# Half slots of a routed expert layer: second product with the tokens as rows, one step later, and both token loads moved among the full slots

## The chip, the cores and the metric

The kernel runs on one core of a Trainium2 chip. The metric is the device time of one execution in microseconds (us). The engines are TensorE (PE, its weight loads PEld), VectorE (DVE), ScalarE (ACT), GpSimd (POOL) and SyncE (SP), which issues nearly all DMAs here. Each engine works through its own queue in the order of the program.

## The reference

Three layers follow one another over 2304 tokens of width 512:

```
attn = softmax(scale*q k^T + bias, causal) v                    # 4 x 8 heads, 576 positions, 64 wide
e    = argmax(x w_gate + modality_bias);  p = softmax(...)[e]   # x: the heads side by side
h    = relu(x[mask] w1[e]);  moe[mask] = p * (h w2[e])          # 8 experts, 512 -> 1024 -> 512
out  = (sigmoid(moe wg) * (moe wv)) wo                          # 512 -> 1536 -> 512
```

With the reference's inputs (seed 0) the router sends 1191 rows to one expert, 1097 to a second, 16 to a third and none to the others.

## The kernel before, in words

**Slots.** After the attention, each expert's rows are cut into full slots of 256 rows; a rest of at most 128 rows becomes a half slot. There are nine full slots (MAIN, the last is slot 8) and two half slots (MAINH, numbered 32 and 33) in the straight path; here that makes five and four full slots and two half slots with 16 and 73 rows, so 2215 rows lie in full slots. More slots than that are done in `extras` (L1070) behind a branch on the register `more`, which the router computes (L822 to L826). `more` is also set when fewer rows than a threshold lie in full slots (L824).

**A full slot** has eight steps (`Moe.step`, L1154), one for each 128 columns of the hidden layer. A step is a first product of 12 matmuls (`mm1`, L989), a Relu on ACT (L993) with the low part `hL` on DVE (L994), and the second product of the step before (`mm2`, L1009). Values are kept as a high and a low part, so that each product is three matmuls. After each step `aheads` splits the weights for three steps ahead (`split_piece`, L922 and L925): two casts on ACT, one subtraction on DVE, one on POOL. Steps are counted from the end of the full slots: step 0 is the first step of the half slots, step -1 the last of slot 8, and each of the negative steps takes about 2.85 us.

**A half slot** has four steps k (`half`, L1111) in plain float32, where the program's one matmul is two passes in the records. A step transposes the hidden part of the step before (`half_t`: PE L1093, copy to `hT` on DVE L1095), makes the first product (`phh`, L1116: eight passes of 256 columns), a Relu on ACT (L1118), and then the second product of the step before (`half_mm2`, L1104: sixteen passes of 128 columns, with the weights `raw` standing in the array and the tokens streaming). The result has the 512 features on the partitions, as the store wants it. After k = 3, `store` (L1015) copies it to `yt` on ACT (L1021) and issues two DMAs on SP: the result to the DRAM tensor `x2` (L1023) and the row numbers to `ids2` (L1031). `half_x` (L1080) transposes the tokens of the next half slot (`htr`), one step of k = 2 of the first or step -2.

**Weights of the half slots.** `load_raw` (L897) loads part a (w1, L902) and part b (w2, L904) of quarter k into the tile pair `raw[k]`. In `Moe.run` (L1190), after half step i, part b of step i - 1 and part a of step i are loaded for the second half slot; a load waits until the product that reads the old contents is done.

**Around the steps.** `main` puts tasks of the third layer (`Moe2`) at steps by `put(step, tasks)`, and `step(u)` runs them after step u. `load_x(t)` (L1258) loads 768 columns of `x2` in four DMAs: t = 0 into tiles `xs`, t = 1 into `xt`. `x_tasks` (L1269, `sums` at L1272) are 18 tasks on such a load: seven casts on ACT (L1277), seven subtractions for low parts (L1278) and four sums (L1279) on DVE. Before, t = 0 is loaded at step -7 and its tasks run three a step at steps -4 to 1; t = 1 is loaded at step 0, and its tasks, with the split of the third layer's first weights (`w_tasks`, L1302 to L1324), run at steps 2 to 8. `preload` (L1242) brings the table for Sigmoid onto ACT, at step 8. Behind step 8 stands the branch over `extras` (L1072), and then `Moe2.run`, which loads t = 2 and starts the third layer's matmuls (L1342).

Of the kernel before, what the change touches and what calls it, by code (L numbers as in the profile page):

```python
# [8 lines left out]
F32 = mybir.dt.float32  # L9
# [6 lines left out]
ALU = mybir.AluOpType  # L16
# [10 lines left out]
BP, BT, WARM = 3, 3, 16  # L27
# [27 lines left out]
class Attention:  # L55
    def __init__(self, tc, ctx, ps, q, k, v, s, ident, new_x, on_batch, tick):
        self.tc, self.nc = tc, tc.nc
        self.q, self.k, self.v, self.s = q, k, v, s
        self.ident = ident
        self.new_x, self.tick = new_x, tick  # L60
        self.on_batch = on_batch
        self.B, self.H, self.S, self.D = q.shape
        self.N = self.B * self.H
        P = lambda n, b, **kw: ctx.enter_context(tc.tile_pool(name=n, bufs=b, **kw))
        self.cp = P("a_const", 1)
        self.wgx = self.cp.tile([128, 4, 144], F32, name="wgx")
        self.wk = P("a_work", 2)
        self.ps = ps
        self.sb = ps.tile([128, 1024], F32, name="sb")
        self.side, self.beside, self.reads = [], None, {}  # L70
        self.in_ctx = ExitStack()
        self.inp = self.in_ctx.enter_context(tc.tile_pool(name="a_in", bufs=2, side="right"))
        self.dr = P("a_dram", 1, space=DRAM)
        self.raw, self.kv, self.hd, self.bias_t, self.oT, self.sums = {}, {}, {}, {}, {}, {}
        self.x, self.pr, self.nr, self.cumB, self.qtt = {}, {}, {}, {}, {}
        self.setup()
# [400 lines left out]
    def run(self, late):  # L477

        pairs = self.N // 2
        last = pairs + max(e[2] for e in PERIOD) - 1  # L480

        def issue(nm, p, par):
            self.emit(nm, p, par)
            if nm[0] in "TALNR" or nm in ("evql", "qksl"):
                self.tick()

        for op in START:
            nm, n = op.split("@")
            issue(nm, int(n) // 2, int(n) % 2)
        for w in range(3, last + 1):  # L490
            for nm, par, sh in PERIOD:
                if 0 <= w - sh < pairs:
                    if (last - w, nm, par) in late:
                        late[last - w, nm, par]()
                    issue(nm, w - sh, par)
# [6 lines left out]
MAINH, HALVES, HROW, NROW = 2, 8, 32, 40  # L502


class Router:
# [240 lines left out]
    def slots(self):  # L746
# [5 lines left out]
        nc, T, q = self.nc, self.T, self.q  # L752
        V = nc.vector
# [4 lines left out]
        cmp, X = (self.fill[:, a : a + 9 * k].rearrange("p (a b) -> p a b", b=9) for a, k in ((0, 8), (72, 4)))  # L758
        A, B, C, nt, inc, E, Z = t9("sA"), t9("sB"), t9("sC"), t9("nt"), t9("inc"), t9("sE"), t9("sZ")
        n1 = lambda nm, dt=F32: T([128, 1], nm, dt)  # L760
        es, ep, s0, el, ch, g1, ex, z, base, void = (n1(nm) for nm in ("es", "ep", "s0", "el", "ch", "g1", "sx", "sz", "base", "void"))
# [3 lines left out]
        op = lambda f, *a, **kw: q.append(lambda: f(*a, **kw))  # L765
# [55 lines left out]
        op(V.tensor_copy, tt, inc[:64, 8:9])  # L821
        op(V.tensor_reduce, s0[0:1], W[0:1, 1], axis=AX.X, op=ALU.add)  # L822
        op(V.tensor_scalar, s0[0:1], s0[0:1], float(MAINH), None, ALU.is_gt)
        op(V.tensor_scalar, void[0:1], X[0:1, 3, 0:1], 4.0 * Moe2.G, None, ALU.is_lt)  # L824
        op(V.tensor_tensor, s0[0:1], s0[0:1], void[0:1], ALU.max)
        op(V.scalar_tensor_tensor, out=more, in0=inc[0:1, 8:9], scalar=float(MAIN), in1=s0[0:1], op0=ALU.is_gt, op1=ALU.max)  # L826
        q.append(lambda: self.indices("idx", self.tid, NROW, self.B * self.S - 1))
# [54 lines left out]
class Moe:  # L882
    def __init__(self, tc, raw, ps, acc, router, w1, w2, x, x2, ids2, ident):
        self.tc, self.nc = tc, tc.nc
        self.acc, self.x2, self.ids2 = acc, x2, ids2
        self.raw, self.ps, self.r, self.w1, self.w2, self.x, self.ident = raw, ps, router, w1, w2, x, ident
        self.xg, self.xT, self.y, self.piece, self.regs = {}, {}, {}, {}, {}
        self.prev, self.hprev, self.pend, self.ready = None, None, [], False
        self.wbufs = 24

    def open(self, ctx, early):
# [163 lines left out]
    def simple_half(self, s):  # L1055
        self.gather(s)
        self.gate(s)
        self.half_x(s)
        for k in range(4):
            self.load_slot(s, k)  # L1060
            self.half(s, k)
        self.half_end()
# [35 lines left out]
    def half_mm2(self, s, k, t):  # L1098
        nc = self.nc
        if k == 0:  # L1100
            self.y[s] = [self.ps.tile([128, 512], F32, tag="tr", name="yh", bufs=BT)]
        for dc in range(4):
            for j in range(2):
                nc.tensor.matmul(  # L1104
                    self.y[s][0][:, 128 * dc : 128 * dc + 128], self.raw[k][1][:, j, 128 * dc : 128 * dc + 128],
                    t[:, 128 * j : 128 * j + 128], start=k + j + dc == 0, stop=k == 3 and j == 1 and dc == 3, skip_group_check=True,
                )
        if k == 3:
            self.store(s)

    def half(self, s, k):  # L1111
        nc = self.nc
        ready = self.half_t(*self.hprev) if self.hprev else None
        ph = self.ps.tile([128, 512], F32, tag="pt", name="phh", bufs=BP)[:, :256]
        for dc in range(4):
            nc.tensor.matmul(ph, self.xT[s][:, dc], self.raw[k][0][:, dc], start=dc == 0, stop=dc == 3)  # L1116
        h = self.wk.tile([128, 256], F32R, tag="hH", name="hh", bufs=4).bitcast(F32)
        nc.scalar.activation(h, ph, AF.Relu)  # L1118
        if ready:
            self.half_mm2(*ready)  # L1120
        self.hprev = (s, k, h)

    def half_end(self):
        self.half_mm2(*self.half_t(*self.hprev))
        self.hprev = None

    LE, LA = 2, 3

# [61 lines left out]
    def run(self, step):  # L1190
        for u in range(8 * EARLY, 8 * MAIN):
            self.next()
            step(u)
            self.aheads(self.LA)
        for i in range(4 * MAINH):
            s, k = HROW + i // 4, i % 4
            self.half(s, k)
            if i == 0:
                self.finish()
                for h in range(1, MAINH):  # L1200
                    self.gate(HROW + h)
            elif k == 2 and s + 1 < HROW + MAINH:
                self.half_x(s + 1)
            for part, j in (("b", i - 1), ("a", i)):
                if 0 <= j < 4 * (MAINH - 1):
                    self.load_slot(HROW + j // 4 + 1, j % 4, part)
            step(8 * MAIN + i)
        ready = self.half_t(*self.hprev)
        self.hprev = None
        self.half_mm2(*ready)  # L1210
        step(8 * MAIN + 4 * MAINH)


# [510 lines left out]
def kernel(ctx, tc, q, k, v, s, modality_id, moe_w_gate, modality_bias, w1, w2, wg, wv, wo, out):  # L1724
    nc = tc.nc
    B, H, S, D = q.shape
    pool = lambda c, n, b=1, **kw: c.enter_context(tc.tile_pool(name=n, bufs=b, **kw))
    cp = pool(ctx, "const")
    dr = pool(ctx, "dram", space=DRAM)
    x = dr.tile([B * S, RW], F32, name="x")  # L1730
# [4 lines left out]
    with tc.manual_schedule():  # L1735
        ident = cp.tile([128, 128], F32, name="ident")
        make_identity(nc, ident)
        ps_ctx, at_ctx, mo_ctx, ea_ctx, mw_ctx, ex_ctx, xs_ctx, wo_ctx, x1_ctx = (ExitStack() for _ in range(9))
# [42 lines left out]
        phase, more, keep = [0], [], []  # L1781
# [19 lines left out]
        glu = Moe2(tc, moe, x2, ids2, wg, wv, wo, out, hd, keep[0], rp, wo32)  # L1801
        todo, last, xs, raws, x1, raws1 = {}, 8 * MAIN, [], [], [], []

        def put(at, tasks):
            todo.setdefault(at, []).extend(tasks)
# [13 lines left out]
        put(-6, [lambda: moe.gate(HROW)])  # L1819
        put(-2, [lambda: moe.half_x(HROW)])  # L1820
        put(0, [mw_ctx.close])
        put(-7, [lambda: glu.load_x(0, raws), lambda: glu.room_x(0, keep[0])])

        def open_second():
            glu.second = pool(ctx, "second", reuse_waits="tile")
            glu.room_x(1, glu.second)
            x1.append(pool(x1_ctx, "x_second", side="right", reuse_waits="tile"))
            raws1.extend(x1[0].tile([128, 2, glu.G], F32, name=f"xt{i}") for i in range(4))
            glu.load_x(1, raws1)

        put(0, [open_second])

        def first_tokens():
            x = glu.x_tasks(0, raws)
            for k in range(6):
                put(k - 4, x[3 * k : 3 * k + 3])

        def later():
            x, cuts = glu.x_tasks(1, raws1), (0, 3, 7, 9, 12, 15, 18, 18)
            w = [[], [], s0[0], s0[1] + s0[2], s0[3] + s0[4], s0[5], s0[6]]  # L1840
            for k in range(7):
                put(2 + k, w[k] + x[cuts[k] : cuts[k + 1]])
            put(8, [glu.preload])

        put(-5, [first_tokens])
        put(1, [later])

        def step(u):
# [51 lines left out]
```

## Time and profile before

| what | us |
|---|---|
| median of 3 runs (lowest to highest) | 951.32 (950.17 to 952.55) |
| the profiled execution, its own time | 945.87 |
| its span, first to last instruction | 944.1 |
| PE busy in that span | 899.6 |

The profile is one execution on one core. "Busy" is time in which an instruction of the engine is under way. A timeline row gives start, duration, engine, line, operation, output and input, how many instructions are merged, and in square brackets how long the engine was idle before and what ended that. In a windows row each engine has its busy time and instruction count in the stretch. Matmul ends are modelled, so that two matmuls in a row overlap a little in the records; distances from start to start show their true rate.

### The profile page before, as it was taken

Reading aid. Unit: us, or ns where it says so; the run is one execution under the profiler, and the core shown is the slowest. Engines: PE = TensorE matmul, PEld = TensorE weight load, DVE = VectorE, ACT = ScalarE, POOL = GpSimd, SP = SyncE. Lnnn points to the kernel's source line nnn. Section 1 sums busy time; section 2 is a strip of 40 time slices with the busy share of each in tenths; the row PEclk is TensorE's granted clock in tenths of the full one; section 3 lists DMA queues with packets and bytes.
Section 4 is the critical chain, followed back from the end, with each engine's and each line's share of the span. In section 5 each row is a group of like instructions: output and inputs, shape, how many; then the busy total and the mean of one; then the engine's idle time right before and its main releaser. Section 6 shows DMA issues by size and latency. Waiting matters only on the chain. (4 is left out here: it accounts for less than half of the span.)

```text
span 944.1 us, 18712 instructions
## 1 busy us (share of the span) xinstructions
PE 899.6 (95%) x6261; PEld 861.0 (91%) x6261; DVE 710.0 (75%) x1583; ACT 554.1 (59%) x1296; POOL 397.2 (42%) x616
## 2 busy tenths in 40 slices
PE   7999999999997999999999899999999999999996
PEld 6899889888887999999998799999999999889996
DVE  6999999999894688867766667767575747878771
ACT  4999899898643665656544455454545344454440
POOL 7988789798742577776630001010000000111111
PEclk8999999999998999999999999999999999999999
DMA  7667559694382355723467322333232308473501
GB/s 173 157 155 161 135 87 128 165 125 145 139 102 69 95 174 180 280 90 90 137 225 242 99 79 95 112 101 120 70 132 76 126 11 296 137 242 111 168 35 44
DMA packets 163903, 125.34 MB, mean 133 GB/s; under 512 B 86737, under 2 KB 147692, under 8 KB 163286
## 3 DMA queue, kind: packets, MB, share of 16 engines
q1 hardware_dynamic: 158790, 113.62, 44.5%
q0 software_dynamic: 3792, 10.14, 3.2%
q8 instruction: 51, 0.84, 0.4%
q14 instruction: 54, 0.44, 0.2%
q10 hardware_dynamic: 1216, 0.30, 0.1%
HBM read 115.95 MB, written 33.23 MB: 158 GB/s over the span
## 5 line engine op out<-in xcount | busy, mean ns | idle before, releaser
L1342 PE MATMUL X<-a,set 128*128 128x384 f32 x864 | 164.7, 338 | 4.8 <-ACTq L1072 3.0
L1342 PEld LDWEIGHTS X<-a,set 128*128 128x128 f32 x864 | 152.4, 188 | 6.6 <-ACTq L1072 3.1
L861 POOL TENSOR_SCALAR dn<-dr 128x256 int8<-128x256 int8 (+1 forms) x60 | 35.2, 588 | 251.3 <-DMA dr<-in_moe_w_gate_dram 96.6
L925 POOL TENSOR_TENSOR w<-raw,w 128x512 fp32r<-128x512 f32 x56 | 79.6, 1431 | 57.2 <-ACT w L922 54.7
L174 POOL TENSOR_SCALAR bias<-cumB,cumT 128x576 f32<-128x576 f32 (+4 forms) x155 | 82.6, 535 | 25.7 <-DVE nm L293 21.3
L1479 POOL DMA_INDIRECT out_dram<-oy,row x18 | 20.0, 1113 | 169.2 <-ACT oy L1503 92.0
L989 PE MATMUL ph<-xT,w 128*128 128x256 f32 x672 | 90.0, 283 | 0.0
L989 PEld LDWEIGHTS ph<-xT,w 128*128 128x128 f32 x672 | 83.6, 188 | 0.0
L1342 PE MATMUL Y<-a,set 128*128 128x384 f32 x432 | 82.0, 338 | 0.0
L302 ACT ACTIVATE P<-P,nm 128x576 f32<-128x576 f32 (+3 forms) x128 | 79.5, 627 | 3.3 <-DVE nm L293 3.2
L337 DVE TENSOR_TENSOR PL<-pt,PH 128x512 fp32r<-128x512 f32 (+1 forms) x128 | 77.0, 629 | 1.9 <-ACT PH L330 1.4
L1342 PEld LDWEIGHTS Y<-a,set 128*128 128x128 f32 x432 | 76.5, 188 | 0.1
L1351 ACT COPY u<-X 128x384 f32<-128x384 f32 x72 | 34.5, 479 | 62.8 <-PE X L1342 62.7
L293 DVE CUSTOM_DVE_ANT_0 P<-sb,bias 128x320 f32<-128x320 f32 (+3 forms) x128 | 67.1, 548 | 2.4 <-PE sb L284 1.9
L330 ACT CAST PH<-pt 128x512 fp32r<-128x512 f32 (+1 forms) x128 | 64.8, 552 | 6.8 <-PE pt L321 5.2
L321 PE MATMUL pt<-ident,P 128*128 128x128 f32 x448 | 64.2, 277 | 3.1 <-DVE PL L337 1.2
L925 DVE TENSOR_TENSOR w<-raw,w 128x512 fp32r<-128x512 f32 x56 | 57.0, 1019 | 11.6 <-ACT w L922 10.8
L922 ACT CAST w<-raw 128x512 fp32r<-128x512 f32 x112 | 63.5, 619 | 0.0
L993 ACT ACTIVATE hH<-ph 128x256 fp32r<-128x256 f32 x72 | 27.7, 384 | 59.7 <-PE ph L989 59.5
L284 PE MATMUL sb<-KT,QH 128*128 128x288 f32 (+3 forms) x192 | 56.3, 317 | 6.6 <-DVE nm L293 4.7
L321 PEld LDWEIGHTS pt<-ident,P 128*128 128x128 f32 x448 | 50.6, 141 | 9.6 <-DVE PL L337 1.9
L1277 ACT CAST hf<-hp 128x768 fp32r<-128x768 f32 x42 | 34.1, 835 | 38.5 <-DVE hp L1279 35.4
(317 smaller groups left out, 2430.9 us busy)
## 6 DMA issues: line engine op xcount, KB each, us to landing
raw<-in_moe_w_dram SPq DMA_DIRECT2D x80, 512.0 KB
h<-sg SPq DMA_DIRECT2D x72, 192.0 KB
cumB<-cum_d SPq DMA_DIRECT2D x32, 288.0 KB
hp<-h SPq DMA_DIRECT2D x24, 384.0 KB
qraw<-in_q_dram SPq DMA_DIRECT2D x58, 128.0 KB
dr<-in_moe_w_out_dram SPq DMA_DIRECT2D x12, 511.6 KB
dr<-in_moe_w_gate_dram SPq DMA_DIRECT2D x24, 255.2 KB
dr<-in_moe_w_val_dram SPq DMA_DIRECT2D x24, 255.2 KB
```

The source lines that it names most:

```text
L174: (nc.vector if n in FILLB else nc.gpsimd).tensor_scalar(res[i][:rows], cumB[:rows, :m], -1.0, self.cumT[:rows, i, n : n + 1], ALU.mult, A ...
L284: nc.tensor.matmul(self.sb[:rows, o : o + c1 - c0], X[:, T0[i] : T0[i] + rows], h["KT"][:, c0:c1], start=j == 0, stop=j == 1)
L293: nc.vector.tensor_tensor_reduce(out=pt[:rows, :m], in0=self.sb[:rows, o : o + m], in1=self.bias_t[n][i][:rows], op0=ALU.add, op1=ALU.min, ...
L302: nc.scalar.activation(h["P"][i][:rows, : T0[i] + rows], h["P"][i][:rows, : T0[i] + rows], AF.Exp, bias=h["nm", i][:rows], scale=-1.0, acc ...
L321: nc.tensor.transpose(pt[:, c : c + 128], h["P"][i][:, T0[j] : T0[j] + 128], self.ident)
L330: self.nc.scalar.copy(t[:, :z], pt[:, :z])
L337: self.nc.vector.tensor_tensor(t[:, :z], pt[:, :z], h["H"][u][:, :z].bitcast(F32), ALU.subtract)
L861: nc.gpsimd.tensor_scalar(o["n"], top(), 56.0, -56.0, ALU.min, ALU.max)
L922: nc.scalar.copy(v, src)
L925: (eng or nc.vector).tensor_tensor(v, src, h.bitcast(F32), ALU.subtract)
L989: nc.tensor.matmul(ph, w[:, 128 * dc : 128 * dc + 128], x[:, dc], start=k == 0, stop=k == 11)
L1342: self.nc.tensor.matmul(bank, w[:, c], a[:, h, c], start=first and k == 0, stop=k == 5, skip_group_check=True)
```

## The change

The second product of a half slot now has the hidden part `hT` standing in the array and the weights streaming, 512 columns at a time: four passes in place of sixteen. Its result has the tokens on the partitions, so it is copied to `xg` on ACT and transposed by four PE instructions (`half_out`) before `store`. It runs two steps behind the first product, not one. After half step i the loads are part b of step i - 2 and part a of step i, and they stand ahead of `finish` (the last second product and the store of slot 8) and of the rest of the step's work. The load of t = 0 goes to step -15 and its tasks to steps -7 to -2; the load of t = 1, with its tiles, goes to step -13, its tasks stay where they were; `preload` goes to step -40. The threshold of rows in full slots that sets `more` rises by 512.

```diff
-        op(V.tensor_scalar, void[0:1], X[0:1, 3, 0:1], 4.0 * Moe2.G, None, ALU.is_lt)
+        op(V.tensor_scalar, void[0:1], X[0:1, 3, 0:1], 4.0 * Moe2.G + 512.0, None, ALU.is_lt)
...
     def half_mm2(self, s, k, t):
         nc = self.nc
         if k == 0:
-            self.y[s] = [self.ps.tile([128, 512], F32, tag="tr", name="yh", bufs=BT)]
+            self.y[s] = self.ps.tile([128, 512], F32, tag="tr", name="yh", bufs=BT)
+        for j in range(2):
+            nc.tensor.matmul(self.y[s], t[:, 128 * j : 128 * j + 128], self.raw[k][1][:, j], start=k + j == 0, stop=k == 3 and j == 1)
+        if k == 3:
+            self.out = s
+            nc.scalar.copy(self.xg[s][:, 0, :512], self.y[s])
+
+    def half_out(self):
+
+        if self.out is None:
+            return
+        s, self.out = self.out, None
+        pt = self.ps.tile([128, 512], F32, tag="tr", name="yt", bufs=BT)
         for dc in range(4):
-            for j in range(2):
-                nc.tensor.matmul(
-                    self.y[s][0][:, 128 * dc : 128 * dc + 128], self.raw[k][1][:, j, 128 * dc : 128 * dc + 128],
-                    t[:, 128 * j : 128 * j + 128], start=k + j + dc == 0, stop=k == 3 and j == 1 and dc == 3, skip_group_check=True,
-                )
-        if k == 3:
-            self.store(s)
+            self.nc.tensor.transpose(pt[:, 128 * dc : 128 * dc + 128], self.xg[s][:, 0, 128 * dc : 128 * dc + 128], self.ident)
+        self.y[s] = [pt]
+        self.store(s)
 
     def half(self, s, k):
         nc = self.nc
-        ready = self.half_t(*self.hprev) if self.hprev else None
+        if self.hprev:
+            self.hready.append(self.half_t(*self.hprev))
         ph = self.ps.tile([128, 512], F32, tag="pt", name="phh", bufs=BP)[:, :256]
...
         nc.scalar.activation(h, ph, AF.Relu)
-        if ready:
-            self.half_mm2(*ready)
+        self.half_out()
+        if len(self.hready) > 1:
+            self.half_mm2(*self.hready.pop(0))
         self.hprev = (s, k, h)
 
     def half_end(self):
-        self.half_mm2(*self.half_t(*self.hprev))
+        self.hready.append(self.half_t(*self.hprev))
         self.hprev = None
+        while self.hready:
+            self.half_mm2(*self.hready.pop(0))
+        self.half_out()
...
             self.half(s, k)
+            for part, j in (("b", i - 2), ("a", i)):
+                if 0 <= j < 4 * (MAINH - 1):
+                    self.load_slot(HROW + j // 4 + 1, j % 4, part)
             if i == 0:
                 self.finish()
...
-            for part, j in (("b", i - 1), ("a", i)):
-                if 0 <= j < 4 * (MAINH - 1):
-                    self.load_slot(HROW + j // 4 + 1, j % 4, part)
             step(8 * MAIN + i)
-        ready = self.half_t(*self.hprev)
-        self.hprev = None
-        self.half_mm2(*ready)
+        self.half_end()
...
-        put(-7, [lambda: glu.load_x(0, raws), lambda: glu.room_x(0, keep[0])])
+        put(-9, [lambda: glu.room_x(0, keep[0])])
+
+        def open_x1():
+            x1.append(pool(x1_ctx, "x_second", side="right", reuse_waits="tile"))
+            raws1.extend(x1[0].tile([128, 2, glu.G], F32, name=f"xt{i}") for i in range(4))
+            glu.load_x(1, raws1)
+
+        put(-15, [lambda: glu.load_x(0, raws)])
+        put(-13, [open_x1])
 
         def open_second():
             glu.second = pool(ctx, "second", reuse_waits="tile")
             glu.room_x(1, glu.second)
-            x1.append(pool(x1_ctx, "x_second", side="right", reuse_waits="tile"))
-            raws1.extend(x1[0].tile([128, 2, glu.G], F32, name=f"xt{i}") for i in range(4))
-            glu.load_x(1, raws1)
...
-                put(k - 4, x[3 * k : 3 * k + 3])
+                put(k - 7, x[3 * k : 3 * k + 3])
...
-            put(8, [glu.preload])
-
-        put(-5, [first_tokens])
+
+        put(-40, [glu.preload])
+        put(-8, [first_tokens])
```

## Rows read from the trace of the kernel before

**Rows 1.** Windows, full slots then half slots' end: stretch, length, busy by engine, clock, DMA share, GB/s.
```profile
447.00:450.00 3.00, 3.00 (x28) 3.00 (x27) 2.05 (x3) 1.57 (x4) 2.44 (x5) 1.00 0.38 118
520.00:525.00 5.00, 2.05 (x17) 1.86 (x17) 0.49 (x2) 2.07 (x3) 0.00 (x0) 1.00 0.24 66
```

**Rows 2.** Timeline of PE in the half slots, up to the third layer's start.
```profile
489.76 1.89 PE L1116 MATMUL phh<-raw,xTh 128*128 128x256 f32 x8
492.92 2.05 PE L1104 MATMUL yh<-hT,raw 128*128 128x128 f32 x16 [1.27 <-DVE hT L1095]
...
495.03 1.89 PE L1116 MATMUL phh<-raw,xTh 128*128 128x256 f32 x8
496.76 1.95 PE L1104 MATMUL yh<-hT,raw 128*128 128x128 f32 x16
498.54 0.60 PE L1086 MATMUL htr<-ident,xg 128*128 128x128 f32 x4
498.98 0.38 PE L1093 MATMUL hth<-ident,hh 128*128 128x128 f32 x2
499.20 1.89 PE L1116 MATMUL phh<-raw,xTh 128*128 128x256 f32 x8
501.64 2.05 PE L1104 MATMUL yh<-hT,raw 128*128 128x128 f32 x16 [0.55 <-DVE hT L1095]
...
518.46 0.38 PE L1093 MATMUL hth<-ident,hh 128*128 128x128 f32 x2
519.94 2.05 PE L1104 MATMUL yh<-hT,raw 128*128 128x128 f32 x16 [1.10 <-DVE hT L1095]
524.94 1.32 PE L1342 MATMUL X<-a,set 128*128 128x384 f32 x6 [2.95 <-ACTq L1072]
```

**Rows 3.** Timeline of ACT: a Relu of the half slots, and the end.
```profile
491.75 0.38 ACT L1118 ACTIVATE hh<-phh 128x256 f32<-128x256 f32 x1 [0.20 <-PE phh L1116]
...
522.07 0.58 ACT L1021 COPY yt<-yh 128x512 f32<-128x512 f32 x1 [3.51 <-issue]
522.67 1.28 ACT L1246 ACT_TABLE_LOAD   x1
527.48 0.48 ACT L1351 COPY p<-X 128x384 f32<-128x384 f32 x1 [3.31 <-SPq L1072]
```

**Rows 4.** The branch's line: queue, instruction, durations ns min/median/max, first and last start.
```profile
L1072 ACTq COMPARE_BRANCH  x1: 54/54/54, 522.1 to 522.1; - x1
L1072 SPq COMPARE_BRANCH  x1: 53/53/53, 523.6 to 523.6; - x1
```

**Rows 5.** Timeline of DVE: steps -6 to -1, and its last copy of hT.
```profile
470.88 0.42 DVE L994 SCALAR_TENSOR_TENSOR hL<-ph,hH 128x256 fp32r<-128x256 f32 x1 [1.15 <-ACT hH L993]
478.56 0.69 DVE L925 TENSOR_TENSOR w<-raw,w 128x512 fp32r<-128x512 f32 x1 [0.29 <-ACT w L922]
479.77 1.51 DVE L1278 TENSOR_TENSOR a<-xs,a 128x768 fp32r<-128x768 f32 x1
484.33 0.95 DVE L1278 TENSOR_TENSOR a<-xs,a 128x768 fp32r<-128x768 f32 x1
...
515.73 0.42 DVE L1095 COPY hT<-hth 128x256 f32<-128x256 f32 x1
519.47 0.42 DVE L1095 COPY hT<-hth 128x256 f32<-128x256 f32 x1
```

**Rows 6.** Timeline of POOL in slot 8, steps -6 to -3.
```profile
470.99 0.69 POOL L962 TENSOR_SCALAR xg<-xg 128x512 f32<-128x512 f32 x1
471.96 1.41 POOL L925 TENSOR_TENSOR w<-raw,w 128x512 fp32r<-128x512 f32 x1 [0.27 <-ACT w L922]
479.18 1.29 POOL L925 TENSOR_TENSOR w<-raw,w 128x512 fp32r<-128x512 f32 x1 [3.02 <-ACT w L922]
```

**Rows 7.** Timeline of PE: the largest wait in the full slots behind the first two.
```profile
387.55 0.39 PE L1009 MATMUL sb<-hL,w 128*128 128x256 f32 x1 [1.38 <-DVE hL L994]
```

**Rows 8.** Windows around a long wait of PE, at 282.8 to 289.1 us.
```profile
290.00:292.00 2.00, 2.00 (x10) 2.00 (x11) 1.29 (x2) 0.00 (x0) 1.25 (x1) 0.50 0.00 1
```

More of the change, by code (lines that the diff above doesn't have):

```diff
@@ L887, in __init__ @@
         self.xg, self.xT, self.y, self.piece, self.regs = {}, {}, {}, {}, {}
-        self.prev, self.hprev, self.pend, self.ready = None, None, [], False
+        self.prev, self.hprev, self.hready, self.out, self.pend, self.ready = None, None, [], None, [], False
         self.wbufs = 24
@@ L1118, in half @@
         nc.scalar.activation(h, ph, AF.Relu)
-        if ready:
-            self.half_mm2(*ready)
+        self.half_out()
+        if len(self.hready) > 1:
+            self.half_mm2(*self.hready.pop(0))
         self.hprev = (s, k, h)
     def half_end(self):
-        self.half_mm2(*self.half_t(*self.hprev))
+        self.hready.append(self.half_t(*self.hprev))
         self.hprev = None
+        while self.hready:
+            self.half_mm2(*self.hready.pop(0))
+        self.half_out()
     LE, LA = 2, 3
```

## The prediction

> **What bounds the kernel now.** I read the windows first, since they show which engine is full in which stage. Through slots 6 to 8 PE is busy for the whole of each stretch, at full granted clock, while DVE and POOL have room (first of [rows 1]). No edit can win time there; it can only lose some. Around the end of the half slots PE is busy 2.05 of 5.00 us (second of [rows 1]), so that is where time lies free. The timeline of PE says what it waits for: three times in the half slots for DVE's copy hT, and at the end for the branch [rows 2]. The timeline of ACT and the branch's line show how the end is put together [rows 3, 4]: ACT's sequencer reaches the branch at 522.1, as soon as the last copy to yt has begun, and PE goes on at 524.94; SP reaches it at 523.6, after the store's DMAs, and the first copy of the third layer, which waits for SP, starts at 527.48. So what dates everything behind the branch is the last copy to yt. A change that brings it forward by some time wins that time, since the third layer then does the same work as before.
>
> I count in two parts: the start of the half slots (before: the full slots), and the distance from there to the last copy to yt.
>
> **Half slots, by starts.** A step without a wait is 0.22 us of transposes (498.98 to 499.20), 1.73 us first product (495.03 to 496.76) and 1.78 us second product (496.76 to 498.54) [rows 2].
> - *Waits that go.* The second product runs a step later, so hT has a whole step more. The three starts come late by 492.92 - 489.76 - 1.73 = 1.43 us, 501.64 - 499.20 - 1.73 = 0.71 us and 519.94 - 518.46 - 0.22 = 1.26 us: -3.40 us.
> - *Fewer passes.* Eight passes of 256 columns take 1.73 us, which is 2048 columns. The new second product streams 4 x 512 = 2048 columns: 1.73 in place of 1.78, eight times, -0.40 us. 512-column float32 passes are not in the trace; if they cost the old rate it is 0, and 128-column passes pay more overhead, not less, so no loss is expected above 0.4.
> - *A new wait.* In the second step nothing stands between the first product and the transposes of its own result in the third (the list holds one entry only). Product 489.76 to 491.49, Relu 491.75 to 492.13 [rows 2, 3]; the transposes come at about 492.18: +0.69 us. Once only, since later steps have a second product in between.
> - *Turning the result.* Two half slots, four transposes each at 0.44 us (498.54 to 498.98). The first lies among other products and costs its 0.44. The last lies on the path, with the copy to xg before it: 0.58 us for a 128x512 copy [rows 3], 0.60 for the transposes' own duration and twice about 0.05 between engines, +1.28 us.
> - *The last hT.* On DVE it came 3.74 us after the one before (515.73 to 519.47), behind tasks of the third layer [rows 5]. In the new order PE has 5.6 us between the two uses (0.22 + 1.73 + 1.73 + 0.22 + 1.73), but the ACT copies to xg and yt of the first half slot now wait for PE in the middle of steps 5 and 6, with casts queued behind them that DVE's tasks need. I take +0.40, bounds 0 and 0.80 (both sides of the 1.26 us wait that is there now).
>
> Sum: -3.40 - 0.40 + 0.69 + 0.44 + 1.28 + 0.40 = **-1.0 us**; with the bounds, between -1.8 (no new wait for the Relu, since ACT has less to do there, or none for the last hT) and -0.2.
>
> **The loads.** Eight x DMAs of 384 KB move to steps -15 and -13, among windows with a DMA share of 0.38 (first of [rows 1]), and the xs and xt tiles are then ready long before their tasks. On SP they stand behind the store of slot 6, whose landing the first waits for, and ahead of one block of third-layer weights and slot 8's weight loads; those have a step or more to spare. I cost this at 0; the cover is that free DMA time, and if it were gone POOL's step (the weights' decode) would be late, and with it the splits. In the half slots the weight loads lose the xt traffic and no longer queue behind slot 8's store, but part b comes a step later. Each has over two steps of 3.7 us before use: 0.
>
> **Preload.** The table load (1.28 us, [rows 3]) leaves the end. It stood between 522.67 and 523.95, while ACT's sequencer was already at the branch (522.1, [rows 4]) and PE came free at 524.94 only; SP, which knows nothing of tables, came later still. Its cover is the branch, and it is worth 0 here. At step -40 ACT has some 1.2 us of room in a step: 0. The Trainium skill, ScalarE: Activation LUTs, section What ACT_TABLE_LOAD costs, puts a switch of tables at about 2.66 us with a drain behind the load; the 1283 ns agree, the drain is not seen here, and by that figure the sum would be an estimated -3.7.
>
> **The tasks in the full slots.** This is the term that decides. Steps -7 to -3 each have hL (0.42) and a weight subtraction (0.69) on DVE and one of 1.3 to 1.4 us on POOL [rows 5, 6]. Nine of the eleven DVE tasks of t = 0, 0.95 us each [rows 5], now come into these five steps; before it was three, the others fell where no weights are split any more. From start to start they take about 0.34, 0.61 and 0.87. By themselves they fit: 5 x 0.95 + 9 x 0.87 = 12.6 us in 5 x 2.85 = 14.2.
>
> But DVE and POOL don't work side by side on such operands. The task at 479.77 took 1.51 us in place of 0.95, and ended 0.87 us after POOL's instruction from 479.18 had ended, at 480.47 [rows 5, 6]: it had waited. The Trainium skill, SBUF: State Buffer, section SBUF: two separate sides, has the rule: DVE operations with two SBUF inputs and GpSimd operations share a port pair that is locked for a whole instruction. By that rule alone, with every POOL instruction in the way, the five steps would hold an estimated 12.6 + 7.2 = 19.8 us.
>
> So I lay the queue out from step -6 at the times of before. hL runs from 470.88; the low part of A22 (second group of three tasks) waits for POOL's gate until 471.68 and ends 472.55; POOL's subtraction (ready 471.96) goes next, to 473.84; the sum to 474.71; the weight subtraction to 475.32; hL of step -5 then starts 1.6 us later than its 473.73 (470.88 + 2.85). PE asks for hL only behind the next first product, so about 2.85 - 0.42 - 0.3 = 2.1 us late are free: no wait yet. Step -5: POOL goes first, to 476.61; three tasks to 479.22, the weight subtraction to 479.83: hL of step -4 is 479.83 - 476.58 = 3.25 late, PE waits 1.15 us. The Relu of step -3 sits on ACT behind casts that wait for the third of those tasks, hL there is some 3.1 late, which the wait already had covers but for 0.1 or 0.2. **+1.3 us.** Bounds: 0, if DVE keeps within its 14.2 us; and +3.9, if POOL's 5 x 1.3 + 0.7 = 7.2 us all come on top of 12.6, less hL's 1.7 (only one SBUF input): 18.1 - 14.2. A wait of this sort and size is in the trace: 1.38 us for hL, at 387.55, where weight decoding filled DVE [rows 7].
>
> **Sum.** -1.0 + 1.3 = +0.3 us, on an execution of 945.87 us (span 944.1). The median of the runs is 951.32, 5.4 above that; the difference carries over, so **951.6 us**, no change. A measurement of this kernel can tell about 0.3%, 2.9 us, from no change: 948.5 to 954.2.
>
> **Rivals.**
> - *The full slots hide the tasks* (0 in place of 1.3). For it: only 88% of five steps is asked of DVE, and in the trace of before its waits are rare. Against it: the row at 479.77. -1.0 us: 950.3.
> - *DVE and POOL alternate without a gap* and the lateness reaches ACT's queue, so that PE waits for hL twice: +3.8 in place of +1.3, net +2.8: 954.1, **slower**. It decides from the point at which hL is over 2.1 us late by step -5 already, which a POOL instruction more ahead of the A22 task would bring. For it: the port rows. Against it: PE waits slow the splits too, and the queue recovers.
> - *The table load is on the path after all*: -1.28 and the small activation behind it, about -1.5 more: 948.8 with the tasks hidden. Against it: [rows 4].
> - *The clock falls.* After a wait of PE of 6.28 us the granted clock was 0.50 afterwards, with 10 matmuls in 2 us [rows 8] against 28 in 3 us (first of [rows 1]); some 6 us of that cost about 3. Now PE has, at the end, about 0.7 us of wait, 0.44 of transposes and then the branch's 2.95 (second of [rows 1], clock 1.00). With the forecast: 954.6.
> - *It doesn't do what it says*: the new threshold sets `more`. With 2215 rows in full slots, above 1536 + 512, it doesn't; if it did, eleven DVE tasks and the reload come on top, over 12 us: 964.
>
> **How the numbers follow.** Forecast 0.40, hidden 0.26, alternating 0.20, table 0.08, clock 0.05, `more` 0.01. Faster by over 0.3%: half of table (0.04) and a fifth of hidden (its terms at their good ends, 0.05), rounded to 0.10. Slower: 0.12 of alternating, 0.03 of the forecast's upper end, 0.04 of clock, `more`: 0.20. The same: 0.70. The range reaches from hidden with the good ends of the half slots (951.3 - 1.8 and half a us of spread) to alternating at its bound (951.3 + 3.9 - 0.2): 949.0 to 955.0.
>
> **What would show it.** Right: no wait for hT at the second products but perhaps a short one at the last; about 0.7 us for the Relu of the second step; the last copy to yt some 31.3 us after the second step's first product (522.07 - 489.76 = 32.3 before); the branch's distances as before; a wait or two for hL of 1 us together in steps -5 to -3, with stretched tasks on DVE. Wrong: PE full through slot 8 (then it is hidden), waits for hL of over 3 us (alternating), a shorter way from the yt copy to the third layer (table), a clock below 1.00 behind 519.

## The result, and the profile after

| what | before | after |
|---|---|---|
| median of the runs, us (lowest to highest) | 951.32 (950.17 to 953.47) | 957.01 (956.01 to 959.46) |
| ratio to before, 95% interval | | 1.007 (1.005 to 1.0089) |
| the profiled execution, its own time | 945.87 | 956.53 |
| its span | 944.1 | 954.8 |
| PE busy | 899.6 | 904.0 |

The kernel is slower by 0.7%, outside the range. The two spans differ by 10.7 us, but 7.1 of those lie ahead of the first store of an expert result (SP L1023, at 296.3 before and 303.4 after), where both programs are the same but for a threshold; in later profiles of the changed kernel that store came at 298.8 and 296.6. So a span against a span misleads. I cut the profiles at marks instead: the first store of the experts, the store of slot 7, the first product of the half slots (`phh`), the last copy to `yt`, and the second group of the third layer (`X`; the first, of six matmuls, needs no copy to leave). Each entry is a difference of two starts, in us.

| profile | first store to slot 7's | slot 8, to `phh` | `phh` to last `yt` | last `yt` to second `X` group |
|---|---|---|---|---|
| before | 170.51 | 19.57 | 35.69 | 5.94 |
| before once more (e1) | 170.97 | 19.56 | 36.31 | 6.52 |
| after | 171.78 | 22.56 | 34.76 | 6.70 |
| changed once more (e5) | 172.30 | 24.07 | 34.77 | 7.21 |
| changed, third (e13) | 172.12 | 23.87 | 34.76 | 6.59 |

Means of three against two: +1.33, +3.94, -1.24, +0.60, together **+4.6 us**. Slot 8 carries most of it.

**Slot 8.** The timeline of PE after, from slot 8 into the half slots and up to the third layer (start, us, line, idle time before and its releaser in brackets):

```profile
484.61 0.39 PE L1009 MATMUL sb<-hL,w 128*128 128x256 f32 x1
...
487.44 0.28 PE L1009 MATMUL sb<-hH,w 128*128 128x256 f32 x1
490.19 0.39 PE L1009 MATMUL sb<-hL,w 128*128 128x256 f32 x1 [2.47 <-DVE hL L994]
...
501.11 1.89 PE L1127 MATMUL phh<-raw,xTh 128*128 128x256 f32 x8
503.54 0.44 PE L1095 MATMUL hth<-ident,hh 128*128 128x128 f32 x2 [0.53 <-ACT hh L1129]
...
526.67 1.88 PE L1105 MATMUL yh<-raw,hT 128*128 128x512 f32 x4
529.05 1.98 PE L1105 MATMUL yh<-raw,hT 128*128 128x512 f32 x4 [0.50 <-DVE hT L1097]
531.76 0.66 PE L1117 MATMUL yt<-ident,xg 128*128 128x128 f32 x4 [0.72 <-ACT xg L1108]
535.91 1.57 PE L1355 MATMUL X<-a,set 128*128 128x384 f32 x6 [3.50 <-PEq L1074]
```

PE now stands 2.47 us for one `hL` in step -4, a stretch that was full before [rows 1]. DVE and POOL around it:

```profile
479.62 1.53 DVE L1291 TENSOR_TENSOR a<-xs,a 128x768 fp32r<-128x768 f32 x1
481.19 1.33 DVE L1292 TENSOR_TENSOR xs<-xs,xs 128x768 f32<-128x768 f32 x1
482.44 1.78 DVE L925 TENSOR_TENSOR w<-raw,w 128x512 fp32r<-128x512 f32 x1
484.15 0.41 DVE L994 SCALAR_TENSOR_TENSOR hL<-ph,hH 128x256 fp32r<-128x256 f32 x1
484.48 2.85 DVE L1291 TENSOR_TENSOR a<-xs,a 128x768 fp32r<-128x768 f32 x1
487.26 1.94 DVE L1292 TENSOR_TENSOR xs<-xs,xs 128x768 f32<-128x768 f32 x2
489.11 0.69 DVE L925 TENSOR_TENSOR w<-raw,w 128x512 fp32r<-128x512 f32 x1
489.71 0.42 DVE L994 SCALAR_TENSOR_TENSOR hL<-ph,hH 128x256 fp32r<-128x256 f32 x1
```

```profile
480.44 1.27 POOL L962 TENSOR_SCALAR xg<-xg 128x512 f32<-128x512 f32 x1
481.70 1.98 POOL L925 TENSOR_TENSOR w<-raw,w 128x512 fp32r<-128x512 f32 x1
483.83 1.36 POOL L949 DMA_INDIRECT xg<-x,idx  x1
485.22 1.29 POOL L925 TENSOR_TENSOR w<-raw,w 128x512 fp32r<-128x512 f32 x1
```

The task at 484.48 is of a kind that took 0.95 us [rows 5]. It took 2.85: it ends 0.82 us after POOL's subtraction from 485.22 ended, at 486.51. So by these rows it had waited for the end of the gather (L949, the tokens of the second half slot) and for the next POOL instruction too; e7 below tests it. The two sums and the weight subtraction follow without a gap, and `hL` of step -4 starts at 489.71.

**The end of the half slots.** The timeline of ACT after shows the table load, now among the full slots, and the end:

```profile
375.47 1.30 ACT L1021 COPY yt<-y 128x512 f32<-128x512 f32 x2
376.79 1.28 ACT L1259 ACT_TABLE_LOAD   x1
378.08 0.20 ACT L1259 ACTIVATE tbl<-tbl 128x1 f32<-128x1 f32 x1
378.19 1.12 ACT L922 CAST w<-raw 128x512 fp32r<-128x512 f32 x2
...
531.12 0.59 ACT L1108 COPY xg<-yh 128x512 f32<-128x512 f32 x1 [3.45 <-PE yh L1105]
532.49 0.59 ACT L1021 COPY yt<-yt 128x512 f32<-128x512 f32 x1 [0.79 <-PE yt L1117]
537.93 0.48 ACT L1364 COPY p<-X 128x384 f32<-128x384 f32 x1 [4.86 <-SPq L1074]
```

The branch's line of after (queue, instruction, durations in ns, first and last start), and under it the row of PE's branch before:

```profile
L1074 ACTq EVENT_SEMAPHORE  x2: 17/17/17, 535.2 to 535.3; - x2
L1074 PEldq EVENT_SEMAPHORE  x2: 51/51/51, 535.5 to 535.7; - x2
...
L1074 PEldq COMPARE_BRANCH  x1: 3682/3682/3682, 531.8 to 531.8; - x1
L1074 ACTq COMPARE_BRANCH  x1: 54/54/54, 532.5 to 532.5; - x1
```

```profile
L1072 PEldq COMPARE_BRANCH  x1: 3897/3897/3897, 520.0 to 520.0; - x1
```

Before, PE met its branch at 520.0 and was through it 3.9 us later, at 523.9, ahead of ACT; what released the third layer was ACT's branch [rows 2, 4]. Now PE's four transposes stand right in front of its branch. It is met at 531.8 and left at 535.5, after ACT's semaphores, and PE releases itself (`PEq` in the row at 535.91), 3.42 us after the last copy to `yt` where it was 2.87. It is close: in e13, the same kernel, ACT came last again and the distance was 3.12.

```profile
530.48 1.76 PE L1355 MATMUL X<-a,set 128*128 128x384 f32 x6 [3.20 <-ACTq L1074]
```

The windows of after (columns as in [rows 1]) show the rest:

```profile
530.00:536.00 6.00, 1.78 (x8) 0.73 (x7) 0.00 (x0) 1.17 (x2) 0.00 (x0) 1.00 0.19 51
536.00:538.00 2.00, 2.00 (x9) 2.00 (x10) 0.00 (x0) 0.07 (x1) 0.00 (x0) 0.68 0.08 16
538.00:540.00 2.00, 2.00 (x8) 2.00 (x7) 0.50 (x2) 0.93 (x2) 0.00 (x0) 0.50 0.32 45
540.00:542.00 2.00, 2.00 (x13) 2.00 (x12) 1.68 (x5) 1.26 (x3) 0.00 (x0) 0.97 1.06 368
```

After a stretch in which PE was busy 1.78 of 6 us, the granted clock is 0.50 (1.2 in place of 2.4 GHz), with 8 matmuls in 2 us against 13 behind it.

### The profile page after: what moved, and what is told of

Its sections match the earlier page's. It is cut to its first block, busy times and chain, and to the rows that moved or that the text cites. A ratio compares the mean times of both kernels' runs of the same rounds, so it can differ in the third digit from the quotient of the medians.

```text
span 954.8 us, 18537 instructions
## 1 busy us (share of the span) xinstructions
PE 904.0 (95%) x6173; PEld 855.4 (90%) x6173; DVE 709.3 (74%) x1583; ACT 555.4 (58%) x1298; POOL 397.4 (42%) x616
## 5 line engine op out<-in xcount | busy, mean ns | idle before, releaser
L360 PE MATMUL ot<-PH,vhl 128*128 128x512 f32 (+3 forms) x160 | 56.0, 360 | 3.8 <-DVE QL L258 3.7
```

## The experiments

**e1, the kernel before against itself; e5, the changed kernel again.** No edits.

> The kernel before, unchanged. Theory (the queue of DVE): of the 10.7 us between the two profiled spans only 2.3 lie behind the store of slot 7 (3.0 lost in slot 8, 0.4 won in the half slots, 0.3 in the third layer); the other 8.4 us lie ahead of it, where the instructions of the two programs are the same, and are mostly chance. Then this run's profile has slot 7's store anywhere between 466 and 476 us, and slot 8 (from that store's DMA to the first half slot's first product) again 19.6 us, the half slots up to the third layer's first matmul again 38.6. Rival (the changed program has a slower start for a reason of its own): the store again at 467 within 1.5 us. Time against before: 1.000, within 0.003.

Measured: 1.0000 (0.9983 to 1.0017). The store of slot 7 came at 467.35, as the rival had it; it is the later profiles of the changed kernel, with the first store at 298.8 and 296.6, that speak for chance in the 7.1 us. The windows of this run behind the branch, and under them one of the kernel before in the profile that the prediction was read from:

```profile
526.00:528.00 2.00, 2.00 (x6) 2.00 (x7) 0.00 (x0) 0.00 (x0) 0.00 (x0) 0.50 0.06 12
528.00:530.00 2.00, 2.00 (x9) 2.00 (x9) 0.00 (x0) 1.00 (x2) 0.00 (x0) 0.65 0.17 18
```

```profile
528.00:530.00 2.00, 1.99 (x11) 2.00 (x12) 1.77 (x4) 1.73 (x4) 0.00 (x0) 1.00 0.62 144
```

So the clock falls in the kernel before as well, in some executions; the profile read for the prediction was one without it.

> The changed kernel, unchanged, beside the runs of the first four experiments. By the stages measured so far: slot 8 +3.0 us, the half slots up to the third layer -0.4 to -0.8, slots 1 to 7 (from the store of slot 0 to that of slot 7) +1.3 to +1.6 because of the preload; theory: together 3.9 us, a ratio of 1.0041, and the 5.7 us of the first comparison held chance of up to 2 us as well. Rival (something more, ahead of the slots): 1.006 or more, and the store of slot 0 later than 296.6 us, where the five other profiles but the first of the changed kernel have it at 294.6 to 296.6.

Measured: 1.0059 (1.0038 to 1.008), between the two expectations; the interval holds both. In this profile the clock was 0.50 behind the branch, and also for some 3 us in slot 8, right behind the wait for `hL`; there slot 8 took 24.07 us.

**e2, the tasks of t = 0 back at steps -4 to 1,** all else as changed.

```diff
-                put(k - 7, x[3 * k : 3 * k + 3])
+                put(k - 4, x[3 * k : 3 * k + 3])
...
-        put(-8, [first_tokens])
+        put(-5, [first_tokens])
```

> The changed kernel with the tasks of t = 0 back at steps -4 to 1 (its load stays at -15). Theory: the tasks met the weight splits on DVE and POOL; slot 8 goes back from 22.6 to 19.6 us, with no wait for hL, the half slots stay at 38.2 or become up to 1.0 longer since their first steps have tasks again; time 3.0 us below the changed kernel's 957.0, 954.0. Rival (the loads' DMAs or SP's queue made slot 8 longer): slot 8 stays at 22.5 and the time at 957.

Measured: 1.0004 (0.9988 to 1.0019). Slot 8 takes 19.57 us again and PE has no wait for `hL` in it, so with the tasks back nothing of slot 8's loss is left. The time fell by more than the 3.0 us that were expected; the ladder below, on one chip, has 2.6 us for this step.

**e3, the half slots alone:** `half_mm2`, `half_out`, `half_end` and the order of the weight loads as changed; loads, tasks, preload and threshold as before.

> The kernel before with the half slots' edits alone (tokens as rows, two steps behind, order of the weight loads), tasks, loads and preload as before. Theory: slot 8 19.6 us, half slots 38.2 (the last copy to yt 0.9 earlier, 0.5 of it lost again at PE's own branch), time 0.4 below before, 950.9. Rival (the half slots cost, by the copy and the transposes at the end): half slots over 39.5, time above 952.

Measured: 1.0004 (0.9989 to 1.002). From `phh` to the last `yt` it took 35.92 us, within what the kernel before takes (35.69 and 36.31): with the load of t = 1 late, casts that wait for `xt` stand on ACT in front of the Relu, and PE waits 0.94 us for it ahead of the fifth step.

**e4, the rest alone:** loads, tasks, preload and threshold as changed, half slots as before.

> The kernel before with the loads, the tasks of t = 0 at -7 to -2, the preload at -40 and the threshold as in the change, but the half slots' products and weight loads as before. Theory: slot 8 22.6 us with a wait for hL of about 2.5; half slots 38.0 or less, as the first wait for hT (DVE busy with tasks) and the one behind the late xt go; time 2.2 above before from these two, 953.5, and 3 more if the slower start belongs to these edits. Rival (the half slots cost): slot 8 19.6 and the time that of before.

Measured: 1.0023 (1.0006 to 1.004). Slot 8 takes 22.56 us. The old half slots take 33.64 us, 2.0 to 2.7 less than before: the waits for `hT` in the second and fourth steps are gone without any change of the second product (the second step's goes with the tasks, the fourth's with the loads: in e16, with early loads alone, 1.27 us of the one stands and the other is gone). In its timeline of PE only the last one is left:

```profile
494.72 1.89 PE L1116 MATMUL phh<-raw,xTh 128*128 128x256 f32 x8
496.45 1.95 PE L1104 MATMUL yh<-hT,raw 128*128 128x128 f32 x16
...
522.84 2.05 PE L1104 MATMUL yh<-hT,raw 128*128 128x128 f32 x16 [1.10 <-DVE hT L1095]
```

Beside these early tasks the new half slots, at 34.76, are the slower ones by 1.1 us.

**e6, the preload alone** at step -40.

```diff
-            put(8, [glu.preload])
...
+        put(-40, [glu.preload])
```

> The kernel before with the preload alone moved to step -40. Theory: it pushes ACT's Relu and casts back in a step that already has a store's two copies and the decoding, and PE waits once more for hL: the stretch from slot 0's store to slot 7's is 171.8 to 172.2 us in place of 170.2 to 171.0, the branch's distances stay, time +1.4 us, 1.0015. Rival (the preload costs nothing there and is worth its 1.5 us at the end): stretch 170.5, last copy to yt to first matmul of the third layer 1.5 shorter, 0.9985.

Measured: 0.9992 (0.9979 to 1.0005), which leaves room for a cost of half a us at most. The trace has one more wait for `hL`, 1.43 us, 10.9 us behind the start of the table load (at 373.11), while one that is always there [rows 7] shrinks from 1.38 to 0.89: 0.9 us net.

```profile
383.98 0.38 PE L1009 MATMUL sb<-hL,w 128*128 128x256 f32 x1 [1.43 <-DVE hL L994]
391.71 0.39 PE L1009 MATMUL sb<-hL,w 128*128 128x256 f32 x1 [0.89 <-DVE hL L994]
```

All eight profiles with the preload at -40 have that wait (1.41 to 1.43), the ten without it do not. The other wait varies by itself (0.72 to 1.41 us in those ten); by the means of all profiles the two together grow by 1.1 us. So the wait is the preload's, but trace and runs don't agree on what it costs. At the end nothing is won: the first `X` comes 2.90 us after the last `yt`.

**e7, the gather of the second half slot at step -8 in place of -5,** else as changed.

```diff
-        if f == 3 and s >= EARLY and s + 2 < MAIN + MAINH:
+        if f == (0 if s == MAIN - 1 else 3) and s >= EARLY and s + 2 < MAIN + MAINH:
```

> The changed kernel with the gather of the second half slot's tokens at step -8 in place of -5. Theory: the low part of A12 lost 1.9 us because POOL's gather and then its subtraction stood in its way; without the gather the subtraction runs up to 1.4 us earlier, the task takes about 1.8 in place of 2.85, hL of step -4 comes a good 1 us earlier, PE's wait for it is 1.0 to 1.5 in place of 2.47 and slot 8 takes 21.2 to 21.6 us. Rival (only the amount of work on DVE counts): wait and slot 8 as before that, 2.5 and 22.5.

Measured: 1.0034 (1.0021 to 1.0048); slot 8 takes 21.41 us. DVE's task (first row) and PE's wait:

```profile
483.50 1.71 DVE L1291 TENSOR_TENSOR a<-xs,a 128x768 fp32r<-128x768 f32 x1
```

```profile
488.06 0.39 PE L1009 MATMUL sb<-hL,w 128*128 128x256 f32 x1 [1.33 <-DVE hL L994]
```

With nothing but the gather gone from this step, the task takes 1.71 in place of 2.85 us and the wait falls by 1.14, the same amount. The gather's part of the loss is shown; what is left, 1.33, is near the 1.15 that the prediction had without it, though `hL` of step -5 came later there than the prediction had it, as with the gather.

**e8, the old orientation, two steps behind,** loads early, tasks at -4 to 1, preload at 8 (no copy to `xg`, no transposes).

> A recombination: second product two steps behind as in the change but with the features as rows as before (no copy, no transposes at the end), both loads at -15 and -13 and the weight loads in the new order, the tasks of t = 0 at -4 to 1 and the preload at 8 as before. Theory: slot 8 19.6 us, stretch of slots 170.5, half slots to the last copy to yt 33.0 to 33.6 with no wait for hT, 2.8 from there to the third layer, time 2.5 to 3 below before: 0.997. Rival (the tokens as rows are what makes the half slots shorter): 35 us and more to the last copy, 1.000.

Measured: 1.0002 (0.9985 to 1.0018), though `phh` to the last `yt` took 33.74 us and the first `X` came 2.89 later, in all some 2 us less than before. Early loads cost part of it ahead of slot 7's store (171.61); the rest lies within what this measurement can tell.

**e9 to e12, fourteen spare matmuls in front of the branch,** so that PE is busy closer to it: on the changed kernel, on the one before, on e8, and on e8 with the loads at -7 and -6.

```diff
+        for _ in range(14):
+            self.nc.tensor.matmul(self.acc[:, :128], self.ident, self.ident, start=True, stop=True)
```

> The changed kernel with 14 spare matmuls of the identity on PE behind the last transposes, ahead of the branch (they compute nothing that is used). Theory (the clock): in the changed kernel PE has 0.5, 0.7 and 3.3 us of waits around its last products and the branch, and in both its profiles the granted clock is 0.50 for 3.4 to 6 us behind it; the spare matmuls, 3.1 us, run while the sequencer fetches behind the branch, so the first matmul of the third layer comes no later (3.2 to 3.5 us after the last copy to yt), the clock stays 1.00, and 1.5 to 2.5 us are won against the changed kernel: a ratio to before of 1.0035 to 1.0045. Rival (the branch alone sets the end, the clock is of no account): ratio 1.0055 to 1.007 as without them, or the first matmul 3 us later.

> The kernel before with the same 14 spare matmuls behind its last second product. The two profiles of it have the clock at 1.00 once and at 0.50 to 0.65 for some 3 us once. Theory: clock 1.00 behind the branch every time, on average 0.5 to 1 us won, ratio 0.999 to 0.9995, and the spread of the runs no wider. Rival: 1.000 or above, as the spare matmuls end behind 524.9 and push the third layer back by up to 0.3 us.

> The two-steps-behind version with the features as rows (tasks and preload as before, both loads at -15 and -13), plus the spare matmuls. By stages: slot 8 19.6 us, to the last copy to yt 33.7, clock 1.00 behind the branch; the loads cost 0.3 to 0.7 us at step -12 (a wait for hL behind the weights' block). Theory: 2.0 to 2.5 us below before, 0.9975. Rival (what is won in the half slots goes elsewhere, as the first run of this version, 1.0002, would have it): 1.000.

> As the run before it, with the loads at steps -7 and -6 in place of -15 and -13, behind the last weights' block. Theory: the wait for hL at step -12 goes (0.3 to 0.7 us less between the stores of slots 0 and 7), slot 8 and the half slots stay, 0.3 to 0.7 us below the run before it, 0.997. Rival (the loads now meet the half slots' weights on the DMA queue): a wait in front of a first product of the half slots, 34.5 us and more to the last copy, no gain.

Measured: 1.0047 (1.0029 to 1.0066), 1.0014 (0.9997 to 1.003), 0.9996 (0.9979 to 1.0012) and 0.9994 (0.9976 to 1.0013). None is measurably faster than the same kernel without them. That they would cost no time in front of the third layer was wrong: the first `X` came 5.2 to 5.5 us after the last `yt` in all four, since PE's branch begins some 1.1 us behind the first of the spare matmuls and so 0.9 us after the last copy, and takes 3.8 to 4.1 us from there. The spare matmuls and PE's branch in e10, whose last copy to `yt` starts at 520.84:

```profile
520.59 3.29 PE L1212 MATMUL sb<-ident 128*128 128x128 f32 x28
```

```profile
L1072 PEldq COMPARE_BRANCH  x1: 3777/3777/3777, 521.7 to 521.7; - x1
```

In e9 PE was still idle for 2.46 us. The clock fell behind it in e10 and e11, not in e9 and e12. No version here is measurably faster than the kernel before.

**e13 to e16, a ladder on one chip,** taking the parts back one after another.

> The changed kernel as it is, the top of a ladder on one chip. By the stages of the profiles the ratio to the kernel before is about 1.0045; by the earlier runs 1.006 to 1.007. I expect 1.005 to 1.006, slot 8 at 22.5 us or more, the last yt copy 34.8 us after the first step's first product of the half slots.

> The changed kernel with the preload back at step 8. If the wait of 0.7 to 1.0 us for hL at step -36 comes from the table load, it is gone, and the ratio is 0.0005 to 0.0009 below the top of the ladder; the table load stands behind the last yt copy, ahead of ACT's branch, and costs nothing there. Rival: the load costs no time in step -36 that isn't won back, ratio the same within 0.0003.

> The kernel of the rung above with the tasks of t = 0 back at steps -4 to 1 as well, so half slots, early loads and threshold are what is left of the change. If the tasks' place costs 3.0 us or more, slot 8 is 19.6 us again and the ratio falls by 0.003 to 0.0045 against the rung above, to about 1.000. Rival: part of the loss lies in the half slots themselves, and the ratio stays at 1.002 or more.

> The kernel before with the early loads of both token blocks and the threshold alone. It tells what the half slots' new orientation is worth beside them. If that brings 0.9 us up to the last yt copy and gives 0.3 to 1.4 us of it back behind it, this kernel and the rung above are within 0.001, both near 1.000. If the new orientation wins by itself, this one is 0.001 or more above the rung; if it loses, as much below. The early loads alone should cost 0.2 to 0.7 us at step -12.

| rung | ratio (95%) | against the rung above | slot 8 | `phh` to last `yt` |
|---|---|---|---|---|
| e13, changed | 1.0047 (1.0028 to 1.0066) | | 23.87 | 34.76 |
| e14, preload back at 8 | 1.0039 (1.002 to 1.0058) | -0.0008 | 23.96 | 34.77 |
| e15, tasks back too | 1.0011 (0.9995 to 1.0027) | -0.0028 | 19.57 | 34.77 |
| e16, half slots back too | 0.9999 (0.9979 to 1.002) | -0.0012 | 19.56 | 35.18 |

On 946.4 us the steps are 0.8, 2.6 and 1.1 us. Each rung's interval reaches some 1.5 to 2 us to either side, so only the whole and the tasks' step, the largest, are firm. That the half slots lose rather than win, and what the preload costs, these times don't show; for the early loads e16 shows no cost, to within 2 us. In the half slots and behind them the stages agree in sign: e16 reaches the last `yt` 0.41 us later than e15, but its second `X` group comes 6.40 after it and not 7.53, since PE passes the branch earlier and the clock is low for less time. The first `X` of the two, e15 first:

```profile
524.79 2.26 PE L1355 MATMUL X<-a,set 128*128 128x384 f32 x6 [3.64 <-PEq L1074]
```

```profile
523.98 1.88 PE L1342 MATMUL X<-a,set 128*128 128x384 f32 x6 [2.88 <-ACTq L1072]
```

The windows of e13 in slot 8 show why it took 23.87 us and not 22.56:

```profile
482.00:484.00 2.00, 0.26 (x1) 0.26 (x2) 2.00 (x4) 1.22 (x2) 0.00 (x0) 0.82 0.48 182
484.00:486.00 2.00, 2.00 (x10) 2.00 (x11) 1.60 (x3) 2.00 (x5) 0.48 (x1) 0.50 0.00 0
486.00:488.00 2.00, 2.00 (x16) 2.00 (x15) 2.00 (x3) 0.39 (x1) 2.00 (x2) 0.83 0.61 182
488.00:490.00 2.00, 2.00 (x20) 2.00 (x19) 0.97 (x3) 0.39 (x1) 0.97 (x1) 1.00 0.85 270
```

Behind the wait for `hL` 10 matmuls run in 2 us where 20 run at full clock. Of the six profiles with that wait of 2.46 or 2.47 us, three have this (e5, e13, e14) and three do not (after, e4, e9); it costs 1.3 to 1.5 us.

## Why the prediction was wrong

**The full slots: the mechanism was right, the term mis-sized.** This is the step that failed most. I gave the tasks +1.3 us, with PE waiting 1.15 us once; slot 8 took 3.0 us more at full clock and up to 4.5 without. My walk through DVE's queue had `hL` of step -5 1.6 us late and that of step -4 3.25. Laid against the times of before (8.36 us later throughout in this profile), `hL` started at 484.15, 2.1 late, and at 489.71, 4.8 late. The walk had POOL's gate (the row of L962) at its old 0.69 us [rows 6]; it ran into DVE's task from 479.62 and took 1.27. And it left out the gather that POOL issues in step -5, so that DVE's next task waited for two POOL instructions in a row, where I had one. The gather stood in the trace of before, between POOL's rows at 471.96 [rows 6] and 479.18:

```profile
473.52 1.09 POOL L949 DMA_INDIRECT xg<-x,idx  x1 [0.15 <-issue]
```

One reading was off as well, without consequence: the task at 479.77 of before ended 0.81 us after POOL's instruction, not 0.87. e7 takes the gather out and gets 1.33 us; e2 takes the tasks out and gets none. The Trainium skill, SBUF — State Buffer, section SBUF: two separate sides, gives the shared ports to the instruction that starts first, for all of it; the row at 484.48 agrees for each POOL instruction, and shows beside it that POOL's next one can go ahead of a DVE instruction that already waits.

My rival with DVE and POOL alternating (0.20, 954.1) was nearest in place and sign, but not what happened: PE waited for `hL` once, not twice. Its sign was `hL` over 2.1 us late by step -5, through a POOL instruction more ahead of the A22 task; `hL` was 2.1 late there, and the instruction more stood a step later. I did not look for it there.

**Half slots: the sum was right, its meaning was not.** To the last copy to `yt` I had -1.0; the profile shows -0.93. Term by term: a first or second product 1.72 to 1.73 us by starts; the new wait for the Relu 0.70 (503.54 - 501.11 - 1.73; I had 0.69); the last turning 1.31 (3.44 from the last second product to the copy, 2.13 before; I had 1.28); the last `hT` 0.66 (I had 0.40, bounds 0 and 0.80). But e4 shows that the moved loads and tasks remove two of the three old waits by themselves, and e3 that the half slots alone win nothing that can be measured (35.92 us to the last `yt`). I credited the second product's delay with what two edits do, and the same waits can't be won twice.

**The branch: wrong.** I took its distance from the last copy as fixed. It was fixed only because ACT came last: PE met its branch 2.1 us ahead of ACT. With the transposes in front PE meets it only 0.7 to 0.8 us ahead, and the branch takes it 3.4 to 3.8 us, so that in seven of the eight profiles with the new half slots and no spare matmuls PE comes last. The first `X` comes 3.11 to 3.58 us after the last `yt` in these eight, and 2.70 to 2.90 in the six with the old orientation: 0.5 us between the means.

**Preload: 0 at the end was right, 0 at its new place is in doubt.** ACT's casts stand behind it (378.19, 1.4 us after the table load began), and PE has a wait for `hL` that no profile without it has; that it runs through later splits on DVE and POOL is argued, not tested. It is 0.9 us net in e6's trace. The ladder gives 0.8 us, less than its intervals, and e6's runs half a us at most, so the cost stays open.

**Loads: nothing that can be measured, but not nothing.** Ten of the twelve profiles with the loads at -15 and -13 have one or two further waits for `hL` in the steps around -12, of 0.2 to 0.8 us each; e16 against before, 0.9999 (0.9979 to 1.002), could not show that much.

**The clock: too small a chance.** I gave it 0.05, on one profile in which it stayed at 1.00. It was 0.50 behind the branch in 14 of the 18 profiles, in programs with old and new half slots alike. From the last `yt` to the second `X` group the old half slots without spare matmuls took 5.9 to 6.5 us, the new ones 6.6 to 7.5: some 0.9 us between the means, clock and PE's later branch (0.5 of it) together. In slot 8 I had not thought of it at all.

**The sum.** By stages +4.6 us, 0.49%; measured 0.70, 0.59 and 0.47% in three runs of the changed kernel. The 0.49% lies inside two of the three intervals and just below the first one's lower end. The mean of the three is 1 us above the stages; that it belongs to a stage that these marks don't see can't be excluded. The tasks' term alone would not have left the range: with 3.9 us in place of 1.3 the forecast is 954.2. What took it out are the terms that I had at 0: 1.3 us ahead of slot 7's store, where the preload's and the loads' waits lie, and 0.6 at the branch.

## What to carry to other kernels

A stage in which PE is full takes no extra DVE work for free: before work is moved there, lay out DVE's and POOL's queues together, step by step, with every instruction that POOL issues (a gather too), and ask what waits if one more of them goes first. Two edits that remove the same wait win it once; run each alone before their gains are added. A distance "fixed" by a branch belongs to the engine that is through it last, and work put in front of an engine's own branch can change which that is.

## What the runs showed of the hardware

- A DVE instruction that waits for POOL can be passed again: 0.95 us became 2.85 behind a gather of 1.36 and a subtraction of 1.29 that started 0.03 us after it.
- A PE wait of 2.46 or 2.47 us was followed by a granted clock of 0.50 in three of six profiles and not in the other three, with the same instructions in that stretch; the idle stretch of PE at the branch (2.8 to 3.7 us, 2.2 to 2.5 with the spare matmuls) in 14 of 18. One profile doesn't tell what a wait costs.
- PE's own branch takes 3.4 to 4.1 us in the 18 profiles. It begins before the matmuls in front of it have ended: in e10 at 521.7, with the spare matmuls from 520.59 to 523.88. ACT's and SP's rows show some 54 ns, and their next instruction, a semaphore's, comes 2.5 to 3.4 us later.
